# A filler unit in calls of 512 tokens, and the second step's scores behind the first step's transposition

## The chip, the core and the metric

The kernel runs on one core of one Trainium2 chip. A core has a matrix engine (TensorE, PE), a vector engine (VectorE, DVE), an activation engine (ScalarE, ACT), a general engine (GpSimd, POOL) and a queue engine that issues most DMAs (SyncE, SP). Each engine runs its own list of instructions in order and waits on semaphores for the others. PE writes its results into PSUM; DVE, ACT and POOL move them to SBUF. The metric is the device time of one execution, in microseconds, as the median of several runs.

## The reference

Three layers follow each other: an attention with a window and 32 global tokens in each of 4 batches, 8 heads of 64; a mixture of 8 experts whose weights come out of eight rounds of row and column normalization; and a dense layer with ELU. Cut to what matters:

```python
# attention: q_l, k_l, v_l (4, 8, 512, 64), q_g, k_g, v_g (4, 8, 32, 64)
out_g = softmax(q_g @ [k_g, k_l].T / 8) @ [v_g, v_l]
out_l = softmax([q_l @ k_g.T / 8, masked(q_l @ k_l.T / 8, |i - j| <= 32)]) @ [v_g, v_l]
x = concat(out_g, out_l) as (2304, 512)
# experts
P = exp(x @ w_gate - max)                      # (2304, 8)
for _ in range(8):
    P /= P.sum(1) + 1e-09; P /= P.sum(0) + 1e-09; P *= 2304 / 8
x = sum(P[:, e:e + 1] * (maximum(x @ w1[e], 0) @ w2[e]) for e in range(8))   # 512 -> 1024 -> 512
# dense layer
h = x @ w_in                                   # 512 -> 2048
return where(h > 0, h, exp(minimum(h, 0)) - 1) @ w_out
```

## The kernel before

**Arithmetic.** Every operand of the two big layers is split into a high and a low half, and a product is three matmuls (`three`, L132 high by high, L134 and L136 with one low half each). An expert's hidden width of 1024 is cut into two units of 512, so there are 16 units u. Most units compute their first layer with seven products of half-size blocks in place of eight (`mix1`, products q1 to q7, L1104 to L1106), which needs sums of blocks of x and of weights: the operands "s1" to "s4" of x, and "t1" to "t4" of the weights (POOL adds them, L752, ACT casts the high half, L756, DVE subtracts the low half, L760). `mix2` is the second layer.

**The attention steps.** Sixteen steps p of one pair of heads and a half batch each run through eight slots i, with a tail step p = 16. A step has its scores (`scores`, L226, the matmuls s<-kq), the maxima and exponentials (`maxi`, DVE L237 and ACT L241, two in each of slots 0, 1, 3 and 4), the transpositions of the weights (`transp`, L247, half in slot 4 and half in slot 6 or 7), the values (`pv`, L262, in the next step), the normalization, and the transposition of the result into x (`x_t`: PE L353, the cast of the high half on ACT L344). In steps 0 and 1 dummy matmuls (`busy`) fill PE.

**The filler.** From step 2 on each slot ends with `fill_for(570 ns)`, which takes matmuls from the generator `filler`: units 0 and 1, which are expert 0, computed in the plain way (`unit_plain`) on the first two batches of tokens, b = 0 and 1. A call of `unit_plain` does a number of tokens: the first layer (`mm1`, tile m1, four hidden blocks of 12 matmuls, each evicted by ACT L140 and DVE L141), then the second (`mm2_part`, tile m2, 128 tokens at a time, 12 matmuls of 512 columns). A matmul is priced at its columns / 2.4 + 3 ns. Unit 0 can only take 256 tokens at a time, since it follows the attention; unit 1 runs behind unit 0.

**Exchange of weights.** Unit 1's weights replace unit 0's in the same buffers, in eight steps (`load_unit(1)`, here `second`): four are taken in the last call of unit 0 (`leave`), four in the first call of unit 1 (`come`, at every 12th element that its first layer yields). While this goes on, `st["swap"]` is true.

**Sums ahead.** The operands s1 to s4 of the first 1024 tokens are prepared in the same time, in eight groups of seven steps (`first_sums`, the deque `ahead`): POOL adds (L455, L458) in the tile acc8, ACT casts into a spare stretch of the tile hh (L474), POOL subtracts (L461), and SP stores both halves to DRAM (L462). One step is taken at each slot, but none while `st["swap"]` is true. Behind the loop all that are left are taken at once; then `x_tg` transposes the global tokens' result and casts it into the same stretch of hh (xtg, L344), and the last logits follow (L383, copied by ACT L388 as lt).

**Behind the attention.** The rest of the filler is run; at every fifth matmul of it one step of the next unit's weight preparation is taken (`pre`), and the routing iterations are taken by planned time (`passed`, `timed`, one every 3900 ns): each is a column sum on PE (L990) and eight small instructions of DVE (L992 to L985). Then the first mix stage begins with product q1 of unit 2.

The program's text sets the order by hand, except that a scheduler may shift instructions on an engine a little.

Of the kernel before, what the change touches and what calls it, by code (L numbers as in the profile page):

```python
# [20 lines left out]
B, H, SL, SG, HD = 4, 8, 512, 32, 64  # L21
# [40 lines left out]
def tile_net(ctx: ExitStack, tc, kq, vw, vc, qg, wg, w1, w2, wi, wo, consts, out):  # L62
# [46 lines left out]
    def xcols(p, k, b):  # L109

        if b < 2:
            return xop[(("11", "12"), ("s4", "22"))[b][k // 2] + p][:, k % 2, :SL]
        return hs[p][:, k, SL:2 * SL] if b < B else hs[p][:, k, 2 * SL:2 * SL + 128]
# [31 lines left out]
    def mm1(w, xs, n, hh, hl):  # L145
        late = None
        for fc in range(4):
            ps = psm.tile([128, 512], F32, tag="m", name="m1")
            for k in range(4):
                f = slice(fc * 128, fc * 128 + 128)  # L150
                yield from three(
                    ps[:, :n], w["1h"][:, k, f], w["1l"][:, k, f], xs("h", k), xs("l", k), k == 0, k == 3,
                )
                if late and k == 0:
                    late()
            late = relu_evac(hh[:, fc, :n], hl[:, fc, :n], ps[:, :n])
            yield "q"
        late()
# [55 lines left out]
    def scores(p):  # L214

        b, h, half = p // 4, p % 2, p // 2 % 2
        t = kq_t[2 * b + h]
        ps = [psr.tile([128, 4, 128], F32, tag="r", name="s") for _ in range(2)]
        for i in range(4):
            for c in range(4):  # L220
                s = 8 * half + 4 * (i % 2) + c
                for r in range(2):
                    rows, k = slice(64 * r, 64 * r + 64), 256 + STARTS[s]
                    q = 32 * s + (NKS if half else 0)
                    a = t[rows, i // 2]
                    nc.tensor.matmul(  # L226
                        ps[r][32 * c:32 * c + 32, i], a[:, q:q + 32], a[:, k:k + 128], start=True, stop=True
                    )
        for r in range(2):
            st[p, r] = dict(  # L230
                ps=ps[r], m=ap3.tile([128, 4], F32, tag="m", name="m"),
                e=ap2.tile([128, 4, 128], F32, tag="e", name="e"),
            )
# [164 lines left out]
        )  # L398
        yield 60.0 * m

    def unit_plain(u, b, c0, swap=None):

        leave, come = (swap is not None and u == v for v in (0, 1))
        hh, hl = (hs[p][:, :, c0:c0 + 256] for p in "hl")
        n = 0
        for r in mm1(wA, lambda p, k: xcols(p, k, b)[:, c0:c0 + 256], 256, hh, hl):
            yield r
            n += 1
            if come and n % 12 == 0:
                next(swap, None)  # L410
        n = 0
        for o in (0, 128):
            i = b * 4 + (c0 + o) // 128
            ps = psm.tile([128, 512], F32, tag="m", name="m2")
            for r in mm2_part(wA, ps, hh, hl, o, range(4)):
                yield r
                n += 1
                if leave and n % 6 == 0:
                    next(swap)
            if u == 0:  # L420
                nc.vector.tensor_copy(accs[i], ps)
            else:
                nc.vector.tensor_tensor(out=accs[i], in0=ps, in1=accs[i], op=ALU.add)
            yield "q"
# [57 lines left out]
    def filler():  # L482
        second = load_unit(1)
        for b in range(2):
            for c0 in (0, 256):
                yield from ready(b, c0)
                unit = unit_plain(0, b, c0, second if b and c0 else None)
                if c0:
                    late = logits(b)
                    yield from takewhile(lambda r: r != "lag", late)  # L490
                    yield from takewhile(lambda r: r != "q", unit)
                    yield from late
                yield from unit
        for b in range(2):
            for c0 in (0, 256):
                yield from unit_plain(1, b, c0, None if b or c0 else second)

    np_ = B * H // 2
    with tc.manual_schedule():
# [55 lines left out]
        for p in range(np_ + 1):  # L555
            live, part, b = p < np_, p % 4, p // 4
            if p == 0:
                scores(0)
                scores(1)
            g_pv = 2 * b + part - 2 if part < 2 and 0 < b else None  # L560
            g_s = 2 * b + part - 2 if part > 1 else None
            g_t = 2 * b - (part == 0) if part in (0, 3) and p else None

            def values():
                pv(p - 1)
                if g_pv is not None:
                    global_pv(g_pv, st[p - 1, 0]["o"][:, 384:384 + VN])
                if g_s is not None and p > 2:
                    scores_g(g_s, st[p - 1, 0]["o"][:, 288:352])

            if live and p > 2:
                scores(p)
            elif p > 0:
                values()
            o0, o1 = (st[p - 1, r]["o"] if p and (p < 3 or not live) else None for r in range(2))
            if p == 2:
                norm(1, 0)
                norm(1, 1)
                x_t(1)
                fill_for(FILL)  # L580
                fill_for(FILL)
                scores(p)
                scores_g(g_s, o0[:, 288:352])
            loads = deque()
            if part < 2 and p:
                loads.append(lambda: load_vc(2 * b + (part - 1 if part else -1)))
            if p % 4 == 0 and 0 < b < B:
                load_qg(b)
            if 0 < p < np_ - 1:
                for j in (0, 2):  # L590
                    loads.append(lambda j=j: load_vw(p + 1, slice(j, j + 2)))
            if live and part < 2 and b:
                for j in range(2):
                    loads.append(lambda j=j: load_kq(2 * b + part, 1, slice(j, j + 1)))
            elif part > 1 and b + 1 < B:
                for j in range(2):
                    loads.append(lambda j=j: load_kq(2 * b + part, 0, slice(j, j + 1)))
            for i in range(8):
                if i == 2 and live and p > 2:
                    values()  # L600
                    o0, o1 = (st[p - 1, r]["o"] for r in range(2))
                if live and i in (0, 1, 3, 4):
                    if i == 4:
                        transp(p, 0)
                    for j in range(2):
                        maxi(p, i // 3, (i % 3) % 2 * 2 + j)
                if p not in (0, 2) and i == (5 if p == 1 else 3 if live else 2):
                    norm(p - 1, 0)
                    norm(p - 1, 1)
                if i == 2 and p == 3:  # L610
                    split(wgs[:, :, :E], wgs[:, :, E:], wgf)
                if i == (5 if live else 3) and g_t is not None:
                    copies = global_t(g_t, o1[:, 384:512])
                if i == (6 if live else 5) and g_t is not None:
                    copies()
                if i == 5 and g_pv is not None:
                    norm_g(g_pv)
                if i == (6 if p > 2 else 3) and g_s is not None:
                    expo_g()
                if i == (7 if p > 2 else 6) and live:  # L620
                    transp(p, 1)
                if p not in (0, 2) and i == (7 if live else 5):
                    x_t(p - 1)
                for _ in range(4 if (p, i) == (1, 7) else 2 if p == 2 and i in (1, 5) else 0):
                    next(unit0_weights)
                if i == 6 and not live:
                    og = psr.tile([128, 512], F32, tag="r", name="og")
                    global_pv(B * 2 - 1, og[:, :VN])
                    norm_g(B * 2 - 1)
                if i > 2:  # L630
                    gated(loads)
                if p == 6 and i < 5:
                    load_raw(1, i)
                if p < 2:
                    busy(WARM if p or i < 4 else 0)
                else:
                    fill_for(FILL)
                if st.get(("xready", 1, 256)) and not st.get("swap"):
                    pop(ahead)
                if p == 13 and i in (0, 4):  # L640
                    logits_part(2)
# [547 lines left out]
    with tc.manual_schedule():  # L1189
# [127 lines left out]
        for k in range(len(turns) + 1):  # L1317
            p, u, f = turns[k] if k < len(turns) else (None,) * 3
# [104 lines left out]
```

## Time and profile before

| | |
|---|---|
| median of 3 runs | 1918.37 us (1917.02 to 1921.85) |
| the profiled execution | 1920.79 us, of which the span shown is 1919.0 |
| PE busy | 98% |
| DVE busy | 75% |
| ACT busy | 40% |
| POOL busy | 33% |

Times in the profile are microseconds from the start of the span. A row of the trace gives the start, the duration, the engine, the line and operation, the tiles out<-in with their shape, and in brackets how long the engine had waited before it and for what. A matmul's duration in such a row is longer than its spacing to the next one, since matmuls overlap; the spacing is read from the starts. The granted clock (PEclk) is the TensorE clock as a share of full speed, 2.4 GHz; 0.5 is its lower level, 1.2 GHz.

### The profile page before, as it was taken

Reading aid. Unit: us, or ns where it says so; the run is one execution under the profiler, and the core shown is the slowest. Engines: PE = TensorE matmul, PEld = TensorE weight load, DVE = VectorE, ACT = ScalarE, POOL = GpSimd, SP = SyncE. Lnnn points to the kernel's source line nnn. Section 1 sums busy time; section 2 is a strip of 40 time slices with the busy share of each in tenths; the row PEclk is TensorE's granted clock in tenths of the full one; section 3 lists DMA queues with packets and bytes.
Section 4 is the critical chain, followed back from the end, with each engine's and each line's share of the span. In section 5 each row is a group of like instructions: output and inputs, shape, how many; then the busy total and the mean of one; then the engine's idle time right before and its main releaser. Section 6 shows DMA issues by size and latency. Waiting matters only on the chain. (4 is left out here: it accounts for less than half of the span.)

```text
span 1919.0 us, 32395 instructions
## 1 busy us (share of the span) xinstructions
PE 1888.2 (98%) x12295; PEld 1629.2 (85%) x12295; DVE 1431.5 (75%) x2739; ACT 768.1 (40%) x1599; POOL 623.7 (33%) x549
## 2 busy tenths in 40 slices
PE   8999999999999999999999999999999999999999
PEld 6777788888888888899999999999999977889997
DVE  4554677766677776787878787888888678788887
ACT  5554233323333323333333333333333245455554
POOL 2045223322323233343535353545455100003322
PEclk9999999999999999999999999999999999999999
DMA  7677512233232323733343333323233495554432
GB/s 247 199 234 222 171 60 66 69 102 126 68 114 69 102 70 96 271 96 125 102 129 96 125 104 117 105 88 105 89 105 105 149 295 173 165 217 132 122 116 72
DMA packets 206940, 250.30 MB, mean 130 GB/s; under 512 B 17344, under 2 KB 154560, under 8 KB 206784
## 3 DMA queue, kind: packets, MB, share of 16 engines
q1 hardware_dynamic: 206784, 248.23, 40.8%
q8 instruction: 97, 1.59, 0.3%
q14 instruction: 59, 0.48, 0.1%
HBM read 189.32 MB, written 58.85 MB: 129 GB/s over the span
## 5 line engine op out<-in xcount | busy, mean ns | idle before, releaser
L136 PE MATMUL m<-w2h,hl 128*128 128x512 f32 x1360 | 532.9, 392 | 1.9 <-DVE hl L1068 1.7
L132 PE MATMUL m<-w2h,hh 128*128 128x512 f32 x1360 | 532.4, 391 | 0.7 <-ACT hh L1072 0.7
L134 PE MATMUL m<-w2l,hh 128*128 128x512 f32 x1360 | 531.9, 391 | 0.0
L1038 ACT ACTIVATE hh<-t 128x288 fp32r<-128x288 f32 (+1 forms) x368 | 184.8, 502 | 433.8 <-DVE t L1032 431.3
L136 PEld LDWEIGHTS m<-w2h,hl 128*128 128x128 f32 x1360 | 255.3, 188 | 58.9 <-DVE hl L1068 4.5
L132 PEld LDWEIGHTS m<-w2h,hh 128*128 128x128 f32 x1360 | 255.6, 188 | 51.3 <-ACT hh L1072 1.6
L134 PEld LDWEIGHTS m<-w2l,hh 128*128 128x128 f32 x1360 | 255.5, 188 | 49.7
L1040 DVE SCALAR_TENSOR_TENSOR hl<-t,hh 128x288 fp32r<-128x288 f32 (+1 forms) x368 | 282.9, 769 | 3.9 <-ACT hh L1038 0.2
L1147 DVE SCALAR_TENSOR_TENSOR acc<-m,pr,acc 128x512 f32<-128x512 f32 x247 | 183.0, 745 | 113.7 <-PE m L136 112.3
L128 POOL TENSOR_TENSOR w2l<-w2r,w2h 128x512 fp32r<-128x512 f32 x120 | 163.2, 1383 | 299.6 <-ACT w2h L124 284.6
L1032 DVE TENSOR_TENSOR t<-q,u 128x288 f32<-128x288 f32 (+1 forms) x348 | 182.8, 526 | 61.5 <-PE q L1106 52.0
L1068 POOL TENSOR_TENSOR hl<-eg,hh 128x288 fp32r<-128x288 f32 (+1 forms) x80 | 56.8, 718 | 332.6 <-ACT hh L1072 298.5
L756 ACT CAST wh<-wt 128x512 fp32r<-128x512 f32 x120 | 68.9, 619 | 234.1 <-POOL wt L752 234.1
L752 POOL TENSOR_TENSOR wt<-w1r,wt 128x512 f32<-128x512 f32 x60 | 89.5, 1491 | 204.5 <-DVE hl L1040 100.9
L752 POOL TENSOR_TENSOR wt<-w1r 128x512 f32<-128x512 f32 x60 | 79.9, 1334 | 156.2 <-DVE hl L1040 125.1
L1087 DVE TENSOR_TENSOR u<-q,s 128x288 f32<-128x288 f32 (+1 forms) x116 | 61.1, 527 | 82.0 <-PE q L1106 59.7
L760 DVE TENSOR_TENSOR wl<-wt,wh 128x512 fp32r<-128x512 f32 x120 | 106.8, 900 | 12.8 <-ACT wh L756 11.0
L1295 DVE TENSOR_TENSOR acc<-m,acc 128x512 f32<-128x512 f32 x105 | 72.1, 687 | 29.8 <-PE m L136 29.7
L826 POOL TENSOR_TENSOR cp<-r,cp 128x512 f32<-128x512 f32 x32 | 42.6, 1331 | 144.0 <-DVE cp L816 73.3
L1085 ACT COPY s<-q 128x288 f32<-128x288 f32 (+1 forms) x116 | 52.0, 448 | 79.2 <-PE q L1106 79.2
L1050 ACT ACTIVATE er<-t 128x288 f32<-128x288 f32 (+1 forms) x96 | 48.5, 505 | 81.5 <-DVE t L1032 81.3
L760 DVE TENSOR_TENSOR wl<-w1r,wh 128x512 fp32r<-128x512 f32 x90 | 80.7, 897 | 0.0
(243 smaller groups left out, 4155.6 us busy)
## 6 DMA issues: line engine op xcount, KB each, us to landing
w1r<-in_w_dram SPq DMA_DIRECT2D x60, 512.0 KB, 4.8
w2r<-in_w_dram SPq DMA_DIRECT2D x60, 512.0 KB, 3.8
vw<-in_vw_dram SPq DMA_DIRECT2D x28, 455.0 KB, 3.9
wh<-wqh SPq DMA_DIRECT2D x98, 128.0 KB, 2.9
wl<-wql SPq DMA_DIRECT2D x98, 128.0 KB, 2.9
r<-in_wo_dram SPq DMA_DIRECT2D x16, 512.0 KB, 3.9
r<-in_wi_dram SPq DMA_DIRECT2D x16, 512.0 KB, 3.8
w2h<-wdh SPq DMA_DIRECT2D x28, 256.0 KB, 3.8
```

What stands on the lines that cost most here:

```text
L128: e.tensor_tensor(out=lo, in0=src, in1=hi.bitcast(F32), op=ALU.subtract)
L132: nc.tensor.matmul(ps, ah, bh, start=first, stop=False)
L134: nc.tensor.matmul(ps, ah, bl, start=False, stop=False)
L136: nc.tensor.matmul(ps, al, bh, start=False, stop=last)
L752: eng.tensor_tensor(out=t, in0=get(a), in1=get(b), op=op)
L756: nc.scalar.copy(wop[n + "h"], v[n] if n[0] == "t" else blk(n))
L760: eng.tensor_tensor(out=wop[n + "l"], in0=src, in1=wop[n + "h"].bitcast(F32), op=ALU.subtract)
L1032: nc.vector.tensor_tensor(out=t, in0=ps, in1=rest, op=ALU.add)
L1038: nc.scalar.activation(hh, t, AF.Relu)
L1040: late.append(lambda: nc.vector.scalar_tensor_tensor(out=hl, in0=t, scalar=0.0, in1=hh.bitcast(F32), op0=ALU.max, op1=ALU.subtract))
L1147: nc.vector.scalar_tensor_tensor(out=accs[i], in0=ps, scalar=scale, in1=accs[i], op0=ALU.mult, op1=ALU.add)
L1295: nc.vector.tensor_tensor(out=acc, in0=ps, in1=acc, op=ALU.add)
```

## The change

Two edits. `unit_plain` gets a parameter m for the number of tokens of a call, and unit 1 is called with 512 in place of 256: two calls instead of four. Its first layer then has 96 matmuls of 512 columns instead of 192 of 256 and 8 evictions of 512 columns on each of ACT and DVE instead of 16 of 256; its second layer is the same. The steps of the exchange of weights stay at every 12th element of the first call. And the scores of step 1 move from before the slots of step 0 to its slot 5.

```diff
-    def unit_plain(u, b, c0, swap=None):
+    def unit_plain(u, b, c0, swap=None, m=256):
 
         leave, come = (swap is not None and u == v for v in (0, 1))
-        hh, hl = (hs[p][:, :, c0:c0 + 256] for p in "hl")
+        hh, hl = (hs[p][:, :, c0:c0 + m] for p in "hl")
         n = 0
-        for r in mm1(wA, lambda p, k: xcols(p, k, b)[:, c0:c0 + 256], 256, hh, hl):
+        for r in mm1(wA, lambda p, k: xcols(p, k, b)[:, c0:c0 + m], m, hh, hl):
...
-        for o in (0, 128):
+        for o in range(0, m, 128):
...
         for b in range(2):
-            for c0 in (0, 256):
-                yield from unit_plain(1, b, c0, None if b or c0 else second)
+            yield from unit_plain(1, b, 0, None if b else second, SL)
...
             if p == 0:
                 scores(0)
-                scores(1)
...
+                if p == 0 and i == 5:
+                    scores(1)
                 if live and i in (0, 1, 3, 4):
                     if i == 4:
                         transp(p, 0)
```

PE at the start of the program; s are scores, ptp transpositions of step 0, o values, idle the dummies:

```order
-L226 MATMUL s<-kq 32x128 x64
-L524 MATMUL idle<-hl 128x512 x4
-L247 MATMUL ptp<-ident,e 128x128 x8
+L523 MATMUL idle<-hl 128x512 x9
+L226 MATMUL s<-kq 32x128 x32
+L523 MATMUL idle<-hl 128x512 x4
+L247 MATMUL ptp<-ident,e 128x128 x4
+L226 MATMUL s<-kq 32x128 x32
+L247 MATMUL ptp<-ident,e 128x128 x4
```

Step 1's 32 score matmuls moved from ahead of all eight transpositions of step 0 to between the first four and the last four (the dummies are the same, with another line number).

ACT at the end of the attention, before the change; xt is the last x tile, acc8 the tile of the sums, lt the copy of the logits, wh a cast of the next unit's weights:

```order
L316 COPY ptg_3269<-pg1_3270 112x512
L344 CAST hh_103<-xt_3294 128x2x256
L474 CAST hh_103<-acc8_115 128x4x128 x2
L344 CAST hh_103<-xtg_3357 128x4x128
L388 COPY lt_3375<-lgp_3366 16x512
L140 ACTIVATE hh_103<-m1_3382 128x256
```

The same place with the change:

```order
L316 COPY ptg_3194<-pg1_3195 112x512
L344 CAST hh_103<-xt_3223 128x2x256
L474 CAST hh_103<-acc8_115 128x4x128 x2
L756 CAST wh_101<-w1r_3431 128x512
L474 CAST hh_103<-acc8_115 128x4x128
L344 CAST hh_103<-xtg_3298 128x4x128
L388 COPY lt_3316<-lgp_3307 16x512
L140 ACTIVATE hh_103<-m1_3322 128x512
```

Three casts of sums stand between the last x tile and xtg, where there were two, and a weight cast between them.

DVE at the start of the first mix stage, before the change; acc7 is the last tile of unit 1, wl low halves of the next unit's weights, and the rows behind are a routing iteration:

```order
L423 TENSOR_TENSOR acc7_114<-m2_3654,acc7_114 128x512
L760 TENSOR_TENSOR wl_102<-wt1_3511,wh_101 128x512
L760 TENSOR_TENSOR wl_102<-wt3_3530,wh_101 128x512
L992 TENSOR_SCALAR pcs_3680<-pcs_3680 128x8
L993 RECIPROCAL pcs_3680<-pcs_3680 128x8
L994 SCALAR_TENSOR_TENSOR pr_68<-pr_68,pcs_3680 128x136
```

The same place with the change:

```order
L423 TENSOR_TENSOR acc7_114<-m2_3510,acc7_114 128x512
L760 TENSOR_TENSOR wl_102<-wt2_3491,wh_101 128x512
L760 TENSOR_TENSOR wl_102<-wt1_3452,wh_101 128x512
L760 TENSOR_TENSOR wl_102<-wt3_3471,wh_101 128x512
L760 TENSOR_TENSOR wl_102<-wt4_3542,wh_101 128x512
L992 TENSOR_SCALAR pcs_3560<-pcs_3560 128x8
L993 RECIPROCAL pcs_3560<-pcs_3560 128x8
```

Four low halves instead of two stand between the last tile of unit 1 and the next iteration.

PE at the last column sums (pcs) of the routing, at the end of that stage, before the change; q5 is the last open product, m2 the next unit's second layer:

```order
L990 MATMUL pcs_3899<-cs_3871,ones_64 128x8
L132 MATMUL m2_3895<-w2h_105,hh_103 128x512
L134 MATMUL m2_3895<-w2l_106,hh_103 128x512
L136 MATMUL m2_3895<-w2h_105,hl_104 128x512
L1104 MATMUL q5_3847<-xs4h_99,wh_101 128x512
L1105 MATMUL q5_3847<-xs4l_100,wh_101 128x512
```

The same place with the change:

```order
L990 MATMUL pcs_3774<-cs_3752,ones_64 128x8
L1104 MATMUL q5_3716<-xs4h_99,wh_101 128x512
L1105 MATMUL q5_3716<-xs4l_100,wh_101 128x512
L1106 MATMUL q5_3716<-xs4h_99,wl_102 128x512
L990 MATMUL pcs_3791<-cs_3783,ones_64 128x8
L132 MATMUL m2_3739<-w2h_105,hh_103 128x512
```

The last column sum came 18 matmuls behind the one ahead of it; now it comes three behind it.

## Rows read from the trace of the kernel before

**Rows 1.** Windows: stretch, length, busy PE PEld DVE ACT POOL, PEclk, DMA share, GB/s.

```profile
59.00:68.00 9.00, 8.68 (x105) 8.11 (x104) 3.89 (x18) 2.91 (x7) 0.09 (x1) 0.62 0.60 199
195.00:203.00 8.00, 7.70 (x42) 7.23 (x43) 2.36 (x5) 1.08 (x4) 1.27 (x1) 0.57 0.97 329
250.00:1919.00 1669.00, 1662.46 (x8725) 1445.23 (x8723) 1293.81 (x2144) 652.25 (x1314) 551.55 (x448) 1.00 0.38 119
```

**Rows 2.** Timeline of the start: PE, ACT and the SP queue.

```profile
6.90 1.86 ACT L241 ACTIVATE e<-e,m 128x128 f32<-128x128 f32 x6 [4.88 <-DVE m L237]
...
9.54 1.16 PE L226 MATMUL s<-kq 64*32 64x128 f32 x64 [3.06 <-DMA kq<-in_kq_dram]
...
11.66 0.82 PE L247 MATMUL ptp<-ident,e 128*128 128x128 f32 x6
11.69 0.33 SPq L195 DMA_DIRECT2D qg<-in_qg_dram  x1
...
13.23 0.62 PE L247 MATMUL ptp<-ident,e 128*128 128x128 f32 x2 [0.76 <-ACT e L241]
13.78 1.41 PE L262 MATMUL o<-vw,pt 128*32 128x65 f32 x64
```

**Rows 3.** Timeline of PE: products of the filler, a wait and the spacing.

```profile
172.19 0.39 PE L132 MATMUL m<-x11h,wh 128*128 128x256 f32 x1 [0.41 <-DVE hl L141]
...
211.09 0.28 PE L132 MATMUL m<-xs4h,wh 128*128 128x256 f32 x1
...
212.53 0.28 PE L132 MATMUL m<-xs4h,wh 128*128 128x256 f32 x1
...
217.06 0.39 PE L132 MATMUL m<-w2h,hh 128*128 128x512 f32 x1
...
218.44 0.39 PE L132 MATMUL m<-w2h,hh 128*128 128x512 f32 x1
```

**Rows 4.** Timeline of PE: global values ahead of the first low clock.

```profile
57.84 0.47 PE L328 MATMUL o<-vc,ptg 112*32 112x65 f32 x17 [2.02 <-issue]
```

**Rows 5.** Timeline of ACT, POOL and PE: the last sums and the logits.

```profile
184.25 0.59 ACT L344 CAST hh<-xt 128x512 fp32r<-128x512 f32 x1 [1.61 <-PE xt L353]
...
185.44 1.28 POOL L461 TENSOR_TENSOR hl<-acc,hh 128x512 fp32r<-128x512 f32 x1 [2.45 <-ACT hh L474]
...
190.69 0.62 ACT L474 CAST hh<-acc 128x512 fp32r<-128x512 f32 x1 [5.33 <-POOL acc L458]
191.39 1.26 POOL L461 TENSOR_TENSOR hl<-acc,hh 128x512 fp32r<-128x512 f32 x1 [0.73 <-ACT hh L474]
...
194.01 0.59 ACT L344 CAST hh<-xtg 128x512 fp32r<-128x512 f32 x1 [2.70 <-DMA sfh<-hh]
...
195.12 0.39 PE L132 MATMUL m<-xs4h,wh 128*128 128x256 f32 x1 [3.80 <-ACT lt L388]
```

**Rows 6.** Timeline of PE, POOL and DVE: the first mix stage.

```profile
222.80 0.40 PE L1104 MATMUL q<-x11h,wh 128*128 128x512 f32 x1
...
224.43 1.61 POOL L752 TENSOR_TENSOR wt<-w1r,wt 128x512 f32<-128x512 f32 x1 [14.51 <-DVE wl L760]
...
229.53 0.15 DVE L992 TENSOR_SCALAR pcs<-pcs 128x8 f32<-128x8 f32 x1
...
231.82 0.68 DVE L1087 TENSOR_TENSOR u<-q,u 128x512 f32<-128x512 f32 x1
...
233.22 0.68 DVE L1040 SCALAR_TENSOR_TENSOR hl<-t,hh 128x512 fp32r<-128x512 f32 x1
233.82 0.69 DVE L1032 TENSOR_TENSOR t<-q,u 128x512 f32<-128x512 f32 x1
...
237.44 0.39 PE L990 MATMUL pcs<-cs,ones 128*128 128x8 f32 x2 [0.75 <-DVE cs L985]
...
247.11 0.39 PE L990 MATMUL pcs<-cs,ones 128*128 128x8 f32 x2 [0.71 <-DVE cs L985]
...
249.52 0.39 PE L132 MATMUL m<-w2h,hh 128*128 128x512 f32 x1
```

## The prediction

> **What bounds the kernel now.** I read the busy time by stretch first, since the change touches only the first 250 us. From 250 us to the end TensorE (PE) is busy for 1662.46 of 1669.00 us [rows 1]: nothing there waits, the change leaves that part's order as it is, and whatever is late at 250 us is late at the end. Before that, the attention steps are filled with matmuls of expert 0, so PE is again the bound, except where it stands still: at the start, where the first scores wait 3.06 us for a load [rows 2]; at 57.84, where it stands 2.02 us for nothing that the profile shows [rows 4]; and 3.80 us at 195.12, behind the last sums of the attention output [rows 5]. After two of these the granted clock falls: its mean is 0.62 in 59 to 68 us and 0.57 in 195 to 203 us [rows 1], about half speed for most of a stretch, which costs 9 x 0.38 = 3.4 us and 8 x 0.43 = 3.4 us. Last I read the first mix stage (222.80 to 249.52 us), where VectorE (DVE) carries both the sums of products and the routing iterations, and PE waits for it twice, 0.75 and 0.71 us [rows 6].
>
> **Start: the second step's scores go behind the first transposition.** PE waits until 9.54 us for the second step's operands and only then transposes the first step's weights, at 11.66 and, after another wait of 0.76, at 13.23; values follow at 13.78 [rows 2]. The first four exponentials are done by 6.90 + 4 x 0.31 = 8.14 us, so four transpositions now lie inside PE's wait, from about 8.2 on. The scores keep their 9.54 (the load sets it) and end at 10.6. The second four transpositions need the last exponentials (about 10.1 on ScalarE, ACT, behind one more copy) and start at 10.65 instead of 13.23; the values can start when their operand is there, about 11.7, since the SP queue's wait at 11.69 [rows 2] ends with that load. 13.78 - 11.7 = 2.1, taken as **-2.2 us** with the warm-up matmuls that fall into the wait; bounds -2.6 (the whole 13.23 - 10.65) and 0 (a later load binds).
>
> **Wider matmuls.** Twelve steps of 256 columns take 212.53 - 211.09 = 1.44 us, 0.120 each; six of 512 take 218.44 - 217.06 = 1.38, 0.230 each [rows 3]. One of 512 in place of two of 256 saves 2 x 0.120 - 0.230 = 0.010 us. There are 96 such places: 48 ahead of the wait at 195, -0.5 us, 48 behind it, **-0.4 us**. A few waits of the kind of 172.19, where a 256-wide product stands 0.41 us for VectorE's low half [rows 3], fall away with half of the evictions: another -0.5 ahead of 195. PE's price for a narrow product, which here is 0.120 - 256/2400 = 0.013 us over its columns' time, is weighed by the Trainium skill, "TensorE: Matmul & The Clock Gate", section "Back-to-back issue gap", at about 2.5 ns a matmul; by it the 96 places would give 0.24 us and not 0.96. The trace's figure is used.
>
> So everything up to the last x tile stands 2.2 + 0.5 + 0.5 = 3.2 us earlier.
>
> **The sums behind it: this gain is swallowed.** While unit 1's weights replace unit 0's, no step of the sums of products' operands is issued. The last four of the eight weight steps are tied to every 12th matmul of unit 1's first call; these are now twice as long, so the sums are let go nine slots later, and at the loop's end 15 steps are left instead of 6. In ACT's order three casts of sums now stand behind the last x cast, where there were two. The rows show what follows: the last x cast at 184.25, the next cast directly behind it; then GpSimd (POOL) subtracts at 185.44, adds again, ACT waits 5.33 us for it and casts at 190.69, POOL subtracts at 191.39; the xtg cast waits 2.70 for the store out of the same tile and starts at 194.01, and PE resumes at 195.12 [rows 5]. One cycle is 191.39 - 185.44 = 5.95 us and depends on itself (sum, cast, subtraction, the same buffers), so an earlier PE does not shorten it. One more of it behind an x cast that is 3.2 us earlier puts PE's resumption at 195.12 - 3.2 + 5.95 = 197.87: **+2.75 us**, and PE's wait grows from 3.8 to about 10. The weight cast that now stands ahead of the third one (L756) waits for a load that is issued two stores earlier and is hidden by the cycle. Bounds 0 (POOL is ahead, nothing left to wait for but one store) and +6 (no gain ahead).
>
> **The clock behind the wait** falls already before: half speed from about 0.8 us after 195.12 to 202.65, mean 0.57 [rows 1]. After a longer wait it can only start low at once: 0, between -1.6 (the low stretch ends sooner) and +0.4 (0.8 us at half speed).
>
> **First mix stage.** Half as many steps in the rest of unit 1 means that the preparation of the next unit's weights, popped every fifth step, comes later, while the routing iterations go by planned time. DVE's order at 222.80 is then: accumulation, four low halves (t2, t1, t3, t4), and only then an iteration, where before one came after two. One full-width instruction takes 233.82 - 233.22 = 0.60 us of DVE, one iteration 231.82 - 229.53 = 2.29 [rows 6]. The fourth low half needs POOL's sum, 1.61 us [rows 6], and a cast, so it ends about 5.05 us after the stage's first product. From there the queue is: iteration to 7.35, four evacuations and one iteration to 12.05, four to 16.75, five to 22.05, six to 27.9, one evacuation's rest and the last to 30.5. PE places a column sum every 18 matmuls, 18 x 0.230 + 0.2 = 4.34 us; against the queue it waits 0.9, 0.4, 0.4, 1.0, 1.6, and for the last, which is now only three matmuls behind its forerunner, 1.65: 5.9 us. The stage is then 102 x 0.230 + 7 x 0.2 + 5.9 = 30.8 us to the next layer's first product, where it was 249.52 - 222.80 = 26.7. By the same queue the order of before gives waits at the two places and of the size that the rows have. **+4.1 us**; bounds 0 (the low halves are done in the idle DVE time ahead of 222.80) and +5.5.
>
> **Sum.** +2.75 - 0.4 + 0 + 4.1 = +6.45. The profiled run took 1920.79 (span 1919.0 and 1.8 around it), 2.42 above the median of the runs, 1918.37; I apply the change to the median: **1924.8 us**; by the profiled run it would be 1927.2.
>
> **Rivals.** *A, not slower: the stall at 57.84 does not recur.* PE stands 2.02 us there on its own issue, and the clock falls behind it [rows 1, 4]. Everything there comes 2.2 us earlier against the same loads; if the two no longer meet, 2.0 + 3.4 = 5.4 us go, ahead of the sums, which then end earlier too. For it: the stall has no releaser in the profile, as a matter of phase would look. Against: the instruction order is unchanged there. 1924.8 - 5.4 = 1919.4. It decides if PE runs through 57.84 - 2.2. *B, not slower: DVE keeps up.* The preparation is done in the 10 us in which PE stands anyway; the two waits of 1.46 us go, the last two iterations, closer together, cost 2.0: +0.5 for +4.1, 1921.2. *C, slower still: the start gains nothing*, because values wait for a load (the 11.69 row speaks for vw's landing just then): 2.2 us come back, 1927.0. *D, not slower: the sums keep pace*, because POOL has finished before the loop's end, so that two casts' time stands behind the last x tile as before: PE resumes 3.2 earlier instead of 2.75 later, 1924.8 - 5.95 = 1918.9. Against D: the rows' 5.33 us in which ACT waits for POOL [rows 5].
>
> **How the numbers follow.** Forecast 0.45, A 0.12, B 0.15, C 0.18, D 0.10. About 0.3% (5.8 us) is what a measurement of this kernel can tell from no change: faster is under 1912.6, slower over 1924.1. The forecast's own spread by the bounds (the start, the clock and the mix stage) puts some 0.3 of its 0.45 over 1924.1, and C nearly all of its share, B and the edge of others a little: slower 0.51. Faster needs A, B and D in part together: 0.05. Same 0.44. The range takes in C and its half of the bounds above, 1930.0, and A and D below, 1917.5.
>
> **What would show it.** PE's wait for the cast of the logits (3.80 before) should be about 10 us and end near 198, with three casts of sums behind the last x cast: if it ends near 192, D holds. The first values should start near 11.7: if at 13.8, C. Column sums (L990) should wait about 6 us in all between 226 and 256: if under 2, B. In 55 to 68 us the clock should be as before: if 1.0, A. Full speed spacing of unit 1's products should be 0.230. The prediction is wrong outright if something in the first 57 us (loads, raw weights) is shifted by the new start, which no row can show.

## The result and the profile after

The changed kernel took 1928.71 us in the median (1926.98 to 1931.51), the kernel before 1918.22 in the runs beside it; the ratio is 1.0052, 95% interval 1.0039 to 1.0065. It is slower, by 10 us, where the prediction had 1924.8 and a range of 1917.5 to 1930.0. The profiled execution was 1926.98 us with a span of 1925.2. Ratios leave out one run of all those told below, of 6443.68 us (of the twelve with seven filler matmuls).

The windows of the trace after, with the columns of [rows 1]:

```profile
59.00:68.00 9.00, 8.68 (x197) 7.57 (x195) 4.71 (x25) 5.06 (x14) 0.45 (x1) 0.97 0.71 242
195.00:203.00 8.00, 7.11 (x25) 5.50 (x26) 2.21 (x4) 1.44 (x3) 0.89 (x1) 0.72 0.91 277
252.00:260.00 8.00, 6.33 (x22) 5.12 (x22) 5.36 (x14) 3.74 (x7) 1.30 (x1) 0.79 0.00 0
262.00:1925.00 1663.00, 1656.64 (x8699) 1440.35 (x8698) 1289.76 (x2137) 646.42 (x1305) 549.25 (x445) 1.00 0.38 119
```

From 262 us on PE is as full as it was. New is the third row: behind the first mix stage the granted clock is low for a while, where it was at full speed. In the first row the clock is nearly full, because the low stretch behind the stall lies ahead of the window here and is short (the mean clock from 56 to 60 us is 0.57); in another execution it is later and longer, as will be seen.

The timeline of the start, which answers [rows 2]:

```profile
5.28 1.16 PE L226 MATMUL s<-kq 64*32 64x128 f32 x64
...
7.40 1.07 PE L247 MATMUL ptp<-ident,e 128*128 128x128 f32 x4
8.41 1.16 PE L226 MATMUL s<-kq 64*32 64x128 f32 x64
9.49 0.66 PE L247 MATMUL ptp<-ident,e 128*128 128x128 f32 x4
10.08 1.41 PE L262 MATMUL o<-vw,pt 128*32 128x65 f32 x64
```

The transpositions stand on both sides of step 1's scores, the values start at 10.08 instead of 13.78, and no row waits for the load that had held the scores for 3.06 us.

The last sums, on ACT and PE, which answer [rows 5]:

```profile
177.87 0.59 ACT L344 CAST hh<-xt 128x512 fp32r<-128x512 f32 x1 [1.06 <-PE xt L353]
179.58 0.62 ACT L474 CAST hh<-acc 128x512 fp32r<-128x512 f32 x1 [1.12 <-DMA sfh<-hh]
185.61 0.62 ACT L474 CAST hh<-acc 128x512 fp32r<-128x512 f32 x1 [5.41 <-POOL acc L458]
186.31 0.62 ACT L756 CAST wh<-w1r 128x512 fp32r<-128x512 f32 x1
191.49 0.62 ACT L474 CAST hh<-acc 128x512 fp32r<-128x512 f32 x1 [4.56 <-POOL acc L458]
194.79 0.59 ACT L344 CAST hh<-xtg 128x512 fp32r<-128x512 f32 x1 [2.68 <-DMA sfh<-hh]
...
195.89 0.80 PE L132 MATMUL m<-xs4h,wh 128*128 128x512 f32 x1 [11.65 <-ACT lt L388]
```

Three casts of sums instead of two stand behind the last x tile, one cycle from 185.61 to 191.49 is 5.88 us, and PE waits 11.65 us instead of 3.80. The weight cast L756 at 186.31 costs nothing, as said. The first mix stage, PE's rows that waited or begin it, and the first products of the next layer, for [rows 6]:

```profile
221.60 0.40 PE L1104 MATMUL q<-x11h,wh 128*128 128x512 f32 x1
...
229.32 0.39 PE L990 MATMUL pcs<-cs,ones 128*128 128x8 f32 x2 [1.12 <-DVE cs L985]
...
244.71 0.36 PE L990 MATMUL pcs<-cs,ones 128*128 128x8 f32 x2 [1.35 <-DVE cs L985]
...
250.90 0.39 PE L990 MATMUL pcs<-cs,ones 128*128 128x8 f32 x2 [1.59 <-DVE cs L985]
...
253.75 0.39 PE L990 MATMUL pcs<-cs,ones 128*128 128x8 f32 x2 [1.67 <-DVE cs L985]
254.00 0.77 PE L132 MATMUL m<-w2h,hh 128*128 128x512 f32 x1
254.56 0.63 PE L134 MATMUL m<-w2l,hh 128*128 128x512 f32 x1
...
257.50 0.40 PE L136 MATMUL m<-w2h,hl 128*128 128x512 f32 x1
257.74 0.39 PE L132 MATMUL m<-w2h,hh 128*128 128x512 f32 x1
```

The stage takes 254.00 - 221.60 = 32.40 us instead of 26.72. Right behind it matmuls of 512 columns start 0.42 us apart (254.56, 254.98, 255.41) until 257.5, and 0.22 to 0.24 from there: the lower clock, which costs about 8 x 0.2 = 1.6 us.

The two profiled executions give 1925.2 - 1919.0 = 6.2 us, the medians 10. The experiments begin with that gap.

### The profile page after: what moved, and what is told of

Read it like the earlier page. It is cut to its first block, busy times and chain, and to the rows that moved or that the text cites. A ratio compares the mean times of both kernels' runs of the same rounds, so it can differ in the third digit from the quotient of the medians.

```text
span 1925.2 us, 32192 instructions
## 1 busy us (share of the span) xinstructions
PE 1887.0 (98%) x12199; PEld 1620.7 (84%) x12199; DVE 1431.8 (74%) x2731; ACT 767.2 (40%) x1591; POOL 624.0 (32%) x549
## 3 DMA queue, kind: packets, MB, share of 16 engines
q8 instruction: 96, 1.57, 0.3%
## 5 line engine op out<-in xcount | busy, mean ns | idle before, releaser
L1040 DVE SCALAR_TENSOR_TENSOR hl<-t,hh 128x288 fp32r<-128x288 f32 (+1 forms) x368 | 284.3, 773 | 3.8 <-ACT hh L1038 0.2
L756 ACT CAST wh<-wt 128x512 fp32r<-128x512 f32 x120 | 68.8, 619 | 237.6 <-POOL wt L752 237.6
```

The costliest lines, as they stand in the source:

```text
L756: nc.scalar.copy(wop[n + "h"], v[n] if n[0] == "t" else blk(n))
L1040: late.append(lambda: nc.vector.scalar_tensor_tensor(out=hl, in0=t, scalar=0.0, in1=hh.bitcast(F32), op0=ALU.max, op1=ALU.subtract))
```

## Experiments

All of them are compared with runs of the kernel before on the same chip; lines of code carry the numbers of the changed kernel, and of the trace in the rows (a variant without the moved lines is off by one or two).

**Each half of the change alone.**

```diff
 # e1: step 1's scores moved, unit 1 in calls of 256 as before
             if p == 0:
                 scores(0)
-                scores(1)
...
+                if p == 0 and i == 5:
+                    scores(1)
```

> Only the move of step 1's scores, unit 1 in calls of 256 as before. Theory (the change loses in three places behind the attention, none of which is the start): the values of step 0 start near 10.1 us instead of 13.78, everything in the filled attention stands 3 to 5 us earlier, two casts of sums stand behind the last x tile as before, the routing order is that of before: 1913 to 1915.5 us, faster by 3 to 5. Rival (the gain of the start is always swallowed by the sums behind the attention): PE resumes at 195 as before, 1918 us.

Measured: 1918.65 us, ratio 0.9996 (0.9986 to 1.0007): no difference, -0.8 us with an interval of -2.7 to +1.3. The profile of it, by contrast, ended 2.9 us earlier than that of before (span 1916.1), with PE resuming at 191.69. Neither theory holds as put: PE does follow the earlier attention, but the gain of the profile is not there in the median, and the profile of before that it is compared with is itself late at its start, as the next question shows.

The other half, `unit_plain(1, b, 0, ..., SL)` with the scores in their old place:

> Only unit 1 in calls of 512; step 1's scores stand where they stood. Theory: the gain of the start is absent, so the last x tile is about 3 us later than with the whole change and so is PE's resumption (near 199 us instead of 195.9); the first mix stage costs the same 5.7 us more than before: 1929 to 1932 us. Rival (PE's resumption doesn't follow the last x tile, it is set by the exchange of weights): same as the whole change, 1927 to 1929 us.

Measured: 1927.15 us, ratio 1.0046 (1.0031 to 1.0062). The calls of 512 carry the whole loss. PE waits 11.83 us for lt and the stage takes 32.39 us, so the two places are as in the full change; but the last x tile is at 176.14, earlier than in the full change and not 3 us later: in this execution the clock stayed full between 54 and 70 us (mean 1.00). The time is that of the rival, its reason is not: PE's resumption follows the last x tile at the same 18.2 us as in the full change. Here, too, the median shows nothing of the move of the scores.

**Is the wait of 3.06 us at the start a property of the kernel?** The kernel before and the changed kernel, unchanged, for a second profile of each.

> The kernel of before, unchanged, for a second profile. Theory (the 3.06 us wait for the second step's operands at 9.54 us is an accident of that one execution, and so was most of the gain that the prediction took from the start): the scores of step 1 run without a wait or with one under 1 us and the values start near 11.8 us, as in the run with 512 tokens alone. Rival (the wait belongs to the kernel): 2.5 to 3.5 us of wait, values near 13.8.

> The changed kernel, unchanged, for a second profile and more times. Theory (of the 10 us between the medians only 6.2 stand in the two profiles; the rest is that other executions have a low granted clock in 55 to 65 us and a later last x tile): 1926 to 1930 us, PE's wait for the logits' copy between 10 and 12 us, mix stage 32.4, ending in a low clock again. Rival (the first profile was typical): 1924.5 to 1926 us by the median of the runs.

The kernel before, PE at the start of its second profile (1919.01 us, span 1917.2):

```profile
7.71 1.16 PE L226 MATMUL s<-kq 64*32 64x128 f32 x64 [0.55 <-DMA kq<-in_kq_dram]
...
9.83 0.82 PE L247 MATMUL ptp<-ident,e 128*128 128x128 f32 x6
11.40 0.62 PE L247 MATMUL ptp<-ident,e 128*128 128x128 f32 x2 [0.76 <-ACT e L241]
11.95 1.41 PE L262 MATMUL o<-vw,pt 128*32 128x65 f32 x64
```

The wait is 0.55 us and the values start at 11.95. The 3.06 belonged to that one execution: of the other two kernels with the scores in their old place, the one with 512 tokens alone has no such wait and the last one below has 1.24, with values at 11.78 and 11.94. In the eight profiles with the move they start between 10.08 and 11.42. In the second profile of the changed kernel the values start at 11.21, so the move is worth 0.7 to 1.9 us there, not 3.7. The changed kernel took 1928.12 us in these runs, ratio 1.0052 (1.0039 to 1.0064), and its second profile, with a span of 1931.0, has this in place of the 2.31 us that the first had at the same instruction:

```profile
59.03 0.75 PE L328 MATMUL o<-vc,ptg 112*32 112x65 f32 x17 [3.91 <-issue]
```

Its window from 56 to 70 us has a mean clock of 0.63, its last x tile is at 183.50 instead of 177.87. So up to the last x tile two executions of one kernel differ by 5.6 us. From that tile on they agree to 0.1 us in each stretch:

| stretch | before | before again | after | after again | difference |
|---|---|---|---|---|---|
| last x cast at | 184.25 | 182.36 | 177.87 | 183.50 | -2.6 on the mean |
| to PE's resumption | 10.87 | 10.85 | 18.02 | 18.04 | +7.2 |
| to the first product of the mix stage | 27.68 | 27.74 | 25.71 | 25.76 | -2.0 |
| to the next layer's first matmul | 26.72 | 26.74 | 32.40 | 32.39 | +5.7 |
| to the span's end | 1669.48 | 1669.51 | 1671.20 | 1671.31 | +1.8 |

The sum, -2.6 + 7.2 - 2.0 + 5.7 + 1.8 = 10.1 us, is the difference of the mean spans of two profiles each, and near that of the medians. The four lower rows agree between the executions; that the first, with its scatter of 5.6 us, brings the sum so near the medians is in part luck. The first profile of after was a lucky one in its first 60 us, that of before an unlucky one.

**The mix stage.** If its cost comes from the place of the iterations, it goes when they stand where they stood. What moved them is this: behind each half of the last two logits 14 steps of the filler are taken outside the loop that counts planned time. By the rows of PE 48 of these 56 are matmuls of the first layer; with 512 columns they are 48 x 0.216 = 10.4 us of plan instead of 48 x 0.110 = 5.3. So 5.1 us less are counted ahead of the mix stage, and with one iteration per 3.9 us one more falls into it: seven column sums instead of six.

```diff
 # e3: the whole change, and
         for b in (B - 1, B):
             for _ in range(2):
                 logits_part(b)
-                for _ in range(14):
+                for _ in range(7):
                     next(fill, None)
```

> The whole change, with 7 instead of 14 filler matmuls taken behind each half of the last logits, so that the routing iterations stand against the products as before (column sums 3, 22, 41, 60, 79, 98 instructions behind the first product of the mix stage, as before). Three casts of sums are still behind the last x tile. Theory (the mix stage costs 5.7 us because the iterations stand one place later, and its last wait costs 1.7 us of clock): the stage takes 26.7 us again instead of 32.4, column sums wait at most 1.5 us in all, PE resumes near 196 as with the change: 1916 to 1919 us. Rival (the stage is late because PE's long wait ahead of it shifts what DVE and POOL do): the stage stays above 31 us, 1924 us or more.

Measured: 1923.44 us, ratio 1.0020 (1.0010 to 1.0031). The stage, PE's rows of it that waited:

```profile
240.78 0.39 PE L990 MATMUL pcs<-cs,ones 128*128 128x8 f32 x2 [0.78 <-DVE cs L985]
...
250.47 0.39 PE L990 MATMUL pcs<-cs,ones 128*128 128x8 f32 x2 [0.76 <-DVE cs L985]
```

It takes 252.87 - 226.12 = 26.75 us, with the two waits that the kernel before has, and no low clock follows, although PE's wait ahead of it is 11.68 us. So the long wait is not the cause. The run alone does not part the place of the iterations from the preparation of the weights: with fewer matmuls taken outside the loop, more steps of the preparation are taken in it as well. The time was missed: I had put PE's resumption at 196, which only the lucky profile showed; it is 199.06 here, from a last x tile at 181.02, and the low clock behind it lasts until 204.5.

Whether the preparation of the weights by itself, which the prediction blamed, holds the iterations up, is asked by taking it earlier with the iterations left in place:

```diff
 # e9: the whole change, and
-            if steps % 5 == 0:
+            if steps % 3 == 0:
                 pop(pre)
```

> The whole change, with the preparation of the next unit's weights taken at every third filler matmul instead of every fifth; the routing iterations and their column sums stand where the change puts them. Theory (the stage is long because the iterations come later and the last two are close together): one low half less ahead of the first iteration, 0.6 us, so the stage takes 31.8 instead of 32.4 us. Rival (the prediction's reason: the late preparation of the weights holds the iterations back): the stage falls to 28 us or less.

Measured: 1928.04 us in one run; the stage takes 254.78 - 222.80 = 31.98 us, with waits of 0.54, 1.35, 1.62 and 1.13 at column sums. Earlier preparation gives back 0.4 us, and the first of the four waits shows it, 0.54 for 1.12. For the others the rows of DVE in the changed kernel decide:

```profile
222.56 1.88 DVE L760 TENSOR_TENSOR wl<-wt,wh 128x512 fp32r<-128x512 f32 x3
226.29 0.69 DVE L760 TENSOR_TENSOR wl<-wt,wh 128x512 fp32r<-128x512 f32 x1 [1.84 <-ACT wh L756]
...
229.78 0.68 DVE L760 TENSOR_TENSOR wl<-w1r,wh 128x512 fp32r<-128x512 f32 x1
```

After the one at 229.78 no low half follows before the stage ends at 254.00, so its last three waits, 4.61 us, do not come from the preparation. The place of the iterations is their cause, with one more of them in the stage.

**The sums.** If the late release of the sums is the other loss, an earlier end of the exchange of weights takes one cycle away.

```diff
 # e4: the whole change, and
-            if come and n % 12 == 0:
+            if come and n % 6 == 0:
                 next(swap, None)
```

> The whole change, with the last four steps of the exchange of weights at every 6th element of unit 1's first call instead of every 12th, so that the sums are let go about as early as before and two casts stand behind the last x tile instead of three. Theory: one cycle of 5.95 us less, PE's wait for the logits' copy 5 to 6 us instead of 11.65, PE resumes near 190; the mix stage keeps its 32.4 us: 1919 to 1923 us. Rival (the long wait is the whole loss): the mix stage falls back to 27 us too, 1914 us or less. Second rival (POOL is the bound of the sums, not their release): PE resumes near 195.9 as with the change, 1927 us.

Measured: 1920.00 us, ratio 1.0005 (0.9996 to 1.0014). PE's two waits ahead of the mix stage are now these:

```profile
183.96 1.31 PE L328 MATMUL og<-vc,ptg 112*32 112x65 f32 x40 [3.38 <-DMA vc<-in_vc_dram]
191.03 0.50 PE L132 MATMUL m<-xs4h,wh 128*128 128x512 f32 x1 [0.47 <-ACT lt L388]
```

From the last x tile (179.92) to PE's resumption are 11.11 us instead of 18.03: the cycle is gone, and POOL was not the bound. The wait was not the 5 to 6 us that I expected: 3.38 of it moved ahead, to the last values of the global tokens, whose load stands on SP behind the stores of sums. The kernel before has 1.05 us there; with the change alone the load is issued ahead of those stores (173.71 against 174.24), and the wait is under 0.4. The mix stage kept its cost, 32.60 us, with the four waits; the two losses are separate.

**Both repairs.**

> The whole change with both repairs: the exchange of weights at every 6th element, and 7 instead of 14 filler matmuls behind each half of the last logits. Theory (two separate losses that add up: one cycle of the sums, 5.95 us, and the mix stage with its clock, 5.7 and 1.7): the mix stage takes 26.7 us, PE resumes near 191 us as with the early exchange alone, which had 1920.0: 1911 to 1914 us, faster than before by 5 to 7. Rival (the time is set by one thing behind both, say the arrival of the next unit's weights): 1918 us or more, with new waits of PE in the mix stage.

Measured: 1914.57 us, ratio 0.9974 (0.9963 to 0.9986), faster than before by 5 us (2.7 to 7.1), a little above what I expected. The stage takes 26.74 us, from the last x tile to PE's resumption are 11.02 us, and no new wait came up in the stage. From the last x tile to the span's end the profile has 1733.0 us, where the two of before have 1734.8 and 1734.9. So some 2 us of the 5 lie behind that tile. The rest lies ahead of it, where executions scatter, and no run here tells what it is made of.

With the exchange at every 4th element (`n % 4`) in place of every 6th:

> As the run before, with the exchange of weights at every 4th element: one cast of sums behind the last x tile instead of two. Theory: the last logits no longer wait for sums, but PE's wait for the global values' load and the last x tile stay: 1909 to 1913 us. Rival (weights of unit 1 or the sums collide with the attention's exponentials on ACT, PE waits for them in 120 to 180 us): 1913 us or more.

Measured: 1913.49 us, ratio 0.9963 (0.9949 to 0.9977). One cast of sums is behind the last x tile, and from it to PE's resumption are 9.41 us. The time is just past the expected range, on the rival's side, and the theory's reason failed: the last logits still wait for a sum. The rival's collision is not seen either, since PE waits in 120 to 180 us as in the other kernels, at most 0.89 us at a time. This is the best version here, ahead of both kernels; it is not told apart from the one before it by their intervals. Its wait for lt is 2.45 us and that for the global values' load 2.11.

And that kernel with step 1's scores back in their old place:

> The kernel with the exchange at every 4th element and 7 filler matmuls, but step 1's scores back ahead of the slots of step 0. Theory (the move is worth the 0.7 to 1.7 us that the first values come earlier, 11.2 or 10.1 against 11.9, and no more): 1914 to 1916 us, about 1 above the kernel with the move, not to be told from it by the interval. Rival (the move gives 3 us as the prediction said): 1916.5 us or more.

Measured: 1913.88 us, ratio 0.9974 (0.9964 to 0.9985), against 0.9963 with the move: the intervals overlap. The move of the scores may be worth something like 1 us; no run here shows that it is worth more than its uncertainty.

## Why the prediction came out as it did

The direction and the two places were right, and the time lay in the range; the size was 6.5 where 10 was measured. The gain of the start rested on one execution's accident, and the reason for the order in the mix stage was in the main another. The terms were off by +0.6, +1.2, -1.6, +1.6 and +1.8 us, so one error made up for part of the others, and that the time still lay in the range is in part luck. Term by term, against the table above:

- **The earlier x tile**, forecast -3.2, is -2.6 on the mean of two executions each, but these scatter by 5.6 us. The start's -2.2 rested on one wait of 3.06 us [rows 2] that a second execution has at 0.55, and the 11.7 at which the values were to be held by a load was no bound, since they start at 10.08 and 11.21; the move alone measured -0.8 (-2.7 to +1.3). I took an execution's accident for the kernel's property. Rival C, that the start gains nothing, stands nearer to the truth than my step, though not by its reason.
- **The sums**, forecast +5.95 from the x tile to PE's resumption, measured 7.2. The extra cycle is 5.88; the other 1.2 us is a wait that I didn't have: the first cast of sums stands 1.71 us behind the x cast (179.58 - 177.87) instead of 0.49 (184.74 - 184.25, the row below), since it now waits for the store of the group before out of the same tile. Rival D, that POOL keeps pace, is out by the 5.41 us in which ACT waits for POOL. The first cast of sums in the kernel before:

```profile
184.74 0.62 ACT L474 CAST hh<-acc 128x512 fp32r<-128x512 f32 x1
```

- **Wider matmuls and the clock behind the wait**, forecast -0.4 + 0, measured -2.0. The saving of columns was right: eleven steps from 208.18 to 210.72 are 0.231 each, as in [rows 3]. The rest is the clock, which I bounded at -1.6 and took at 0: PE resumes at the low clock at once and leaves it near 199.4, after 3.5 us, where before it ran 0.9 us at full speed and then 6.8 us low. Half of the difference of 3.3 us is 1.7. The clock fell at 189.2 us, while PE stood, so part of the low stretch passed in the wait. Windows of two microseconds of the trace after:

```profile
195.00:197.00 2.00, 1.11 (x3) 0.92 (x4) 0.84 (x2) 0.84 (x2) 0.89 (x1) 0.50 0.68 155
197.00:199.00 2.00, 2.00 (x6) 1.57 (x5) 0.44 (x1) 0.00 (x0) 0.00 (x0) 0.50 0.92 311
199.00:201.00 2.00, 2.00 (x11) 1.39 (x10) 0.22 (x1) 0.00 (x0) 0.00 (x0) 0.90 1.02 290
```

The clock column is at half from the resumption on and nearly full over the window from 199.

- **The first mix stage**, forecast +4.1, measured +5.7. The queue on DVE came out in the order that I wrote down, and the waits in the size: the four rows above add up to 5.73 us, forecast were 5.9. The term that was too small is PE's own time: 32.40 - 5.73 = 26.7 us, where the sum had 102 x 0.230 + 7 x 0.2 = 24.9 (in the kernel before it is 26.72 - 1.46 = 25.3, with two stops instead of four). So a stop seems to cost PE more than the wait in its row (an estimate from these sums); what the rest is, no row names. DVE was later to the same degree, 7.7 us instead of 7.35 at the first stop and 32.1 instead of 30.5 at the last; most of its full-width instructions stand 0.60 us apart as I took them, two of L1040 0.70 and 1.11. The reason that I gave for the order was in the main wrong: the fifth-step preparation is 0.4 us of it (e9), the rest comes from the wider matmuls that planned time doesn't count (e3).
- **Behind the stage**, forecast nothing, measured +1.8. Four waits of 1.1 to 1.7 us in 25 us, the last two 2.9 us apart, are followed by the low clock at 254.00, for 3.4 us; in the repaired kernels, with two waits of 0.75 to 0.78, the clock stays full. I had looked at the clock only where it already fell before. The Trainium skill, "TensorE: Matmul & The Clock Gate", section "Why this matters for your kernels", warns of idle gaps between bursts of matmuls as a cause of such a fall, but of single gaps longer than any of these. The trace agrees that the fall follows gaps, and differs in their size: here each was at most 1.67 us.

Rival A, that the stall near 57 us goes, is out: 2.31 and 3.91 us in the two executions. The low clock behind it lasts 3.4 us in the first of them (56.0 to 59.5) and 10.2 in the second (58.5 to 68.8), against 6.8 in both of before, so the short one is no gain of the change. Rival B, that DVE keeps up, is out by the 5.73 us of waits at column sums.

What stays open: why the instruction at 57 us waits 2 to 4 us for its own issue, and why the clock falls behind it in some executions and not in others. The kernel with 512 tokens alone waits 1.97 us there and keeps full speed, the second profile of before waits 1.97 and does not. No run was made for it, as all kernels here share it.

## What to carry to other kernels

Count, beside an instruction's cost, everything that is paced by the number of instructions: here two schedules (a step at every twelfth matmul, a fixed number of matmuls outside the clock of the plan) doubled in time when the matmul did, and the stretches that they delayed lost 7.2 + 5.7 + 1.8 = 14.7 us, where the wider matmul saves 0.96 by its spacing. Both were cured by halving the count, and the kernel that was 10 us slower is then about 5 us faster than before. And before a wait in one profile is put into a sum, see it in a second execution: a wait for a load in the first microseconds may be that execution's own.

## What the runs showed of the hardware that was not expected

- From the last x tile on, two executions of one kernel agreed within 0.2 us over more than 1700 us, for the kernel before and for the changed one. What they differ by, 1.9 and 5.6 us at that tile, is made ahead of it, mostly by the loads at the start (second scores waiting 3.06 or 0.55 us), by the length of the stall near 57 us (1.97 to 3.91 us in the twelve profiles) and by the low clock behind it, which lasts 6.8 us in eight of them, 3.4 in one, 10.2 in one, and is missing in two.
- Waits of 1.12, 1.35, 1.59 and 1.67 us within one stage were followed by 3.4 us at the lower clock. With the early exchange and with the early preparation the clock fell behind the third wait (1.57 and 1.62 us) and stayed low for 6.8 us. In the seven profiles with two waits of 0.71 to 1.15 us in that stage it did not fall.
- A longer wait can be cheaper by its clock: behind 11.65 us of standing still the low clock lasted 3.5 us more, behind 3.80 us it lasted 6.8. The length of the wait alone does not set it: it was 5.4 us behind 11.68 (seven filler matmuls) and 3.3 us behind 3.38 (early exchange).
